# A fused attention and token-mixing kernel: a new table for the order of issue and for who copies

## The chip, the core and the metric

The kernel runs on one core of a Trainium2 chip. A core has a matrix engine (PE, with weight loads shown apart as PEld), a vector engine (DVE), a scalar engine (ACT), GpSimd (POOL), and a queue on SyncE (SP) that starts the transfers. Each engine works through its own instructions strictly in the order in which they were issued, and semaphores tie the engines together. The metric is the time of one execution on the device in microseconds (us). The kernel before took 118.97 us in the median of three runs (117.5 to 119.05).

## The reference

```python
# q, k, v: (8, 8, 576, 64) float32; w_q, w_k: (512, 64); w_out: (512, 512)
def phi(x, c, s):                        # c, s: cos and sin of pi/2 * position / 576
    r = np.maximum(x, 0.0)
    return np.concatenate([r * c, r * s], axis=-1)
q_p, k_p = phi(q, cos_w, sin_w), phi(k, cos_w, sin_w)
kv  = np.einsum('bhsf,bhsd->bhfd', k_p, v)
z   = np.sum(k_p, axis=2)
x   = np.einsum('bhsf,bhfd->bhsd', q_p, kv) / (np.einsum('bhsf,bhf->bhs', q_p, z)[..., None] + 1e-6)
x   = x.transpose(0, 2, 1, 3).reshape(8, 576, 512)
W   = (1 / 8) * np.einsum('bsd,btd->bst', x @ w_q, x @ w_k)
out = np.maximum(np.einsum('bst,btd->bsd', W, x), 0.0) @ w_out      # float32, (8, 576, 512)
```

## The kernel before

The eight batches are cut into sixteen half batches H of four heads. Everything is written out by hand: a table of words, `ORDER`, is read from front to back, and each word issues one step. A word has the step's name, its number, after a colon the bank of the accumulator memory (PSUM, eight banks; for output copies the number of one of sixteen output buffers), and after an @ the engine: A is ACT, V is DVE, G is POOL. So `RQ2@A` is the relu of q for half batch 2 on ACT. A final a or b means one half of the step's data. An engine's order is the order of its words; words on different engines bind each other through data and buffers alone.

The steps of a half batch H:

- LV, LK, LQ load v, k and q, 288 KB for each half (line 137, SP); four buffers for each of the three.
- RK, RQ: relu and cast of k and q (line 202 on ACT, 204 on POOL). CV: cast of v (208 on ACT, 210 on POOL). VS: v times the cos and sin tables, on DVE from CV's result (line 236) or on POOL straight from the loaded v (line 233).
- KV or KU: the product of k and v on PE (lines 258 and 284), KE copies it out (lines 208 on ACT, 212 on DVE).
- QT or QU: transposition of q on PE, in 18 narrow or 9 wide matmuls (lines 269 and 276); QM multiplies it by the tables on DVE (lines 303 and 300, the latter twice for each QU).
- N (two for each H): numerators and denominators on PE (line 319). EJ adds epsilon, RC takes the reciprocal (line 338), X divides on DVE (line 344, two for each H).
- XT or XR: x transposed on PE, in 10 wide or 20 narrow matmuls (lines 367 and 380); XE copies it out. On ACT this copy moves two bf16 at a time as one float32 word; on DVE it moves bf16.

The steps of a batch b: WK and WQ project x (lines 403 and 416), KW and QW copy the results; KX multiplies by x (line 506), XK copies the result out, XA and XB copy it across the two halves of the partitions (each 64x256). MX (four for each batch, two matmuls, line 535) mixes the tokens, ME applies the relu (line 526 on ACT, 528 on DVE). Batches 4 and 5 go through a joint variant (WC, QC, WT, KC, KP, XP, MP, MM). For two batches together there are nine output tiles: WO is four matmuls of 512 columns (line 552), OE copies the bank out (208 on ACT, 212 on DVE), ST stores 256 KB (line 562, SP).

At the start stand the tables: TQ, TK and TI on POOL, TV and TW (sine by ACT, lines 167 and 182; TV makes the small table for v, TW the one for q), TP and T2 copy TV's table (lines 172 and 186), TZ sets edges of buffers to zero in eight memsets (lines 190 to 195). LW loads and CW casts the weights.

v's scaled copies have two buffers, so VS of H waits for KV of H-2; the loads wait for the relu or cast that empties their buffer.

Of the kernel before, what the change touches and what calls it, by code (L numbers as in the profile page):

```python
# [21 lines left out]


ORDER = """
LV1a LK1a LQ1b LV1b TI TQ TZ0@G TK LQ1a TV T2 TP0 CV1a@A RQ1b@G TW LK1b RQ1a@A CV1b@G VS1a@V
VS1b@V RK1a@G RK1b@A QT1:0 LV0a LQ0b LQ0a LV0b LK0a LK0b LV2a LV2b CV0a@A LK2a LK2b LQ2b QM1 LQ2a
KV1:2 CV0b@G KE1@A LQ3b LQ3a LW0 LW1 N3:2 LV3a LV3b N2:0 LK3b VS0a@V LK3a LV4b LV4a VS0b@V RQ0a@A
LQ4a RQ0b@A RK0a@G LQ4b RK0b@G EJ1@A LK4a LQ5a LK4b LQ5b LW2 CV2@G LV5a LW3 LW4 LW5 LV5b LK5b
LK5a RC1 QU0:4 KV0:6 QM0 KE0@A X2 X3 N1:6 RK2@G N0:4 EJ0@A VS2@V RQ2@A RC0 XR1:2 XE1@A RQ3@G X0
KU2:0 QT2:4 X1 XT0:6 XE0@A CW1@A KE2@V QM2 QU3:0 CW0@V N5:4 N4:6 CV3@G RK3@G QM3 LV6b LQ6a LV6a  # L30
LK6b LQ6b VS3@V EJ2@V WK0:2 KW0@A WQ0:3 QW0@A KX0:2 RC2 X5 LK6a KV3:0 XK0@A XA0@A VS4@G MX1:2
XB0@A KE3@A ME1@A RQ4@A X4 MX0:4 ME0@V LV7b N6:0 N7:2 RQ5@G EJ3@V MX3:6 XT2:4 ME3@A RK4@A RC3
QT4:6 X7 XE2@A X6 XT3:0 KV4:2 KE4@A QM4 XE3@V QU5:6 WK1:0 N8:2 QM5 CW2@G CW4@G CW5@G KW1@A MX2:4
N9:0 EJ4@V CW3@G ME2@A RC4 CV5@G KX1:6 WQ1:7 X8 WO3:4 WO2:5 QW1@A XK1@A WO1:6 X9 VS5@V OE2:0@V
OE1:1@V XB1@A OE3:2@A XA1@A MX6:0 RK5@G MX5:4 KV5:2 ME5@V ME6@A MX7:6 MX4:0 KE5@A LQ7a ME7@A LV7a
LK7b LQ8a LQ7b ME4@V LV8b LK7a N10:2 N11:4 LV8a LQ8b EJ5@V RC5 XR4:6 WO0:0 WO6:1 X10 XE4@A CV6@G
RQ6@G RK6@G WO5:6 X11 QU6:4 OE0:3@A OE5:4@A OE6:5@A VS7@G VS6@V QM6 KV6:2 XT5:6 WO8:1 KE6@V XE5@V
N12:2 N13:4 WO7:0 RQ7@A OE8:6@V EJ6@V RC6 WK2:1 RK7@A KW2@A RQ8@A LV9a LK8b LQ9b LK8a LV10b LQ9a
QT7:6 X13 LV9b OE7:7@V LK9b LK9a LV11b LQ10b LQ10a QM7 WQ2:4 LV10a LQ11a LK11b LK10b LK10a LQ11b
LV11a KV7:0 LK11a KE7@A VS8@G QU8:6 X12 KX2:5 N15:2 XK2@A RK8@A N14:0 QM8 EJ7@V WO4:5 RC7 X14  # L40
KU8:6 X15 XB2@G XA2@G OE4:8@A QW2@A KE8@A MX8:4 MX9:0 ME8@A ME9@V XR6:2 RQ9@G XR7:6 XE7@V QU9:0
XE6@A N16:4 N17:6 WK3:2 WQ3:3 QM9 RK9@A KW3@A VS9@G EJ8@V RC8 RQ10@A KX3:2 XK3@A XB3@A MX10:0
QW3@A X16 KU9:4 KE9@A X17 ME10@V MX11:2 MX15:0 N19:4 N18:6 ME11@A ME15@V WO11:2 EJ9@V XA3@A
MX12:0 WO12:3 RC9 X18 LQ13b LV13b RK10@A LV13a LK12a LQ12b LK13a LQ13a MX13:6 LV12b LK14a LK14b
LK12b ST2 ST6 LV12a LK13b LQ12a X19 MX14:4 OE12:9@V OE11:10@A ME12@A VS10@G KV10:0 ME13@A ME14@V
XR9:2 XE9@V RQ11@G QT11:6 QT10:4 QM10 KE10@A RK11@A XT8:0 XE8@A QM11 WO16:2 VS11@G WO15:3 N20:0
OE15:11@A N21:4 EJ10@A OE16:12@V KV11:6 RC10 X21 RQ13@G WO13:2 KE11@A N22:6 X20 N23:4 WO14:3
EJ11@V WO9:0 OE13:13@A LV15a ST12 LV14b ST3 LK15b ST15 LQ14b LV15b RC11 OE14:14@A XR10:2 LK15a
LQ14a LQ15b ST8 ST13 ST5 ST16 LQ15a X23 X22 QT13:4 OE9:15@A XR11:6 XE11@V WC4:0 XE10@A WC5:6
VS13@G QC4@A QC5@V WO17:0 RQ12@A QT12:2 WT2:6 RK13@A KC2@A WO10:1 KP2:6 OE17:0@V QM13 KV13:4  # L50
OE10:5@A XP2@A KE13@A MP22:6 MP20:0 QM12 MP23:2 RK12@G VS12@G MM22@A KV12:4 MP19:6 MM23@A MM20@V
VS15@G MP16:0 KE12@V MP21:2 MM16@V MM19@A MM21@A N24:4 N25:6 MP18:0 EJ12@A MM18@A WO26:2 OE26:9@A
ST14 LV14a ST17 WO21:0 RC12 X25 X24 N26:2 MP17:6 N27:4 OE21:2@A WO25:0 MM17@V EJ13@A RQ14@A RC13
RK15@G X26 OE25:11@V X27 ST7 ST21 RQ15@G RK14@G WO24:6 WO22:2 OE24:6@A VS14@G KV15:6 QT15:4
OE22:13@V ST22 ST4 ST26 ST1 ST0 QT14:2 QM15 KE15@A QM14 XR13:6 WO19:0 WO18:1 XE13@A XR12:6 N30:4
N31:2 OE19:4@A XE12@V EJ15@V OE18:12@A KV14:0 KE14@A WK6:6 RC15 X31 X30 N29:0 N28:2 KW6@A WQ6:6
KX6:7 EJ14@V QW6@A XK6@A WO23:4 XA6@G RC14 X29 X28 XR14:2 XR15:6 XE14@A XB6@A MX24:0 OE23:14@V
WO20:5 ME24@A XE15@V WK7:4 KW7@A MX27:2 OE20:0@V ME27@A MX26:0 MX25:6 ME25@V ME26@A WQ7:5 KX7:4
XK7@A QW7@A XB7@G XA7@A WO29:0 WO27:1 MX30:4 OE29:7@V MX28:6 MX31:2 WO30:0 OE27:2@A ME28@A ME31@V
ST18 ST24 ST25 MX29:6 ST10 ST9 ST23 ME29@A ME30@V ST11 WO28:1 WO34:6 ST27 ST29 ST20 OE28:13@V  # L60
OE30:8@A OE34:9@A ST19 WO35:0 WO33:1 WO31:6 OE31:1@A ST30 ST28 WO32:4 ST34 OE35:3@V OE32:12@A
ST35 OE33:6@V ST33 ST31 ST32
"""


# [566 lines left out]
```

## Time and profile before

| | |
|---|---|
| median of 3 runs | 118.97 us |
| the profiled execution | 119.31 us, span 117.0 us, mean granted PE clock 0.978 |
| busy in the span | PE 95.5, PEld 63.4, DVE 87.5, ACT 68.7, POOL 74.3 us |
| moved by the transfers | 39.36 MB, 336 GB/s over the span; 29.62 MB read, 9.44 MB written |
| chain that ended last | PE 67%, transfers 11%, DVE 6%, ACT 4% |

The span is the time from the first to the last instruction; the execution's own time is 2.3 us longer. Rows of groups give the line, the engine, the operation, what it writes and reads, the count, the busy time and the mean of one in ns. Rows of a timeline give the start, the duration, the engine, the line and the operation, and in brackets how long the engine sat idle ahead of it and what released it. Rows of the chain give start, duration and what the end was waiting for then.

### The profile page before, as it was taken

To read this page: it belongs to the slowest core of one execution; us is meant where nothing else is said; L and a number is where in the kernel's file an instruction comes from. 1 tells how busy PE (TensorE), PEld (TensorE's weight loads), DVE (VectorE), ACT (ScalarE), POOL (GpSimd) and SP (SyncE) were. 2 spreads that over 40 slices of the span, in tenths; PEclk is the share of its full clock that TensorE was granted. 3 is DMA by queue.
4 is the path that set the end of the run, shared out by engine and by line. 5 is a ranking of instruction groups with operands and counts; after the bars stand their busy time and mean duration, and the time that the engine had idled before them with its cause. 6 is when DMAs were issued, how large, how long until landed. Compare 5 with 4: busy or idle time off the path is not lost.

```text
span 117.0 us, 4959 instructions
## 1 busy us (share of the span) xinstructions
PE 95.5 (82%) x2124; PEld 63.4 (54%) x2138; DVE 87.5 (75%) x132; ACT 68.7 (59%) x120; POOL 74.3 (63%) x72
## 2 busy tenths in 40 slices
PE   0018746998799999988887988999999999999970
PEld 0017544875684657675754555484555668563420
DVE  0336897898989899988795986948779899846330
ACT  4457215359736656748788944469786454585540
POOL 7461670579876779879999955999499950110000
PEclk9999998599999999999999999999999999999997
DMA  3999999999999999999999999999993179731994
GB/s 99 294 387 412 392 384 330 380 391 390 389 392 390 391 385 385 381 388 384 395 384 391 390 385 387 395 393 385 397 391 137 52 277 370 269 124 49 381 382 174
DMA packets 20660, 39.36 MB, mean 336 GB/s; under 512 B 3232, under 2 KB 3232, under 8 KB 20640
## 3 DMA queue, kind: packets, MB, share of 16 engines
q1 hardware_dynamic: 20640, 39.07, 91.0%
q8 instruction: 16, 0.26, 0.9%
q14 instruction: 4, 0.03, 0.1%
HBM read 29.62 MB, written 9.44 MB: 334 GB/s over the span
## 4 chain that ended last, share of the span: by engine, by line
PE 67%; DMA 11%; DVE 6%; issue 5%; ACT 4%; SPq 4%; DVEq 0%; ACTq 0%
PE ps L552 27%; PE ps L319 8%; DMA qraw<-in_q_dram 6%; DMA vraw<-in_v_dram 5%; PE ps L258 5%; SPq L137 4%; DVE x L344 3%; PE ps L380 3%; PE ps L276 3%; PE ps L367 3%; PE ps L403 3%; PE ps L506 3%; PE ps L535 3%; PE ps L269 3%; PE ps L416 3%
## 5 line engine op out<-in xcount | busy, mean ns | idle before, releaser
L233 POOL TENSOR_TENSOR v<-vraw,vtab 128x1152 bf16<-128x1152 f32 x20 | 42.1, 2130 | 4.7 <-PE ps L258 3.1
L552 PE MATMUL ps<-wow,mix 128*128 128x512 bf16 x130 | 33.4, 380 | 1.2 <-DVE o L212 0.4
L344 DVE TENSOR_TENSOR x<-ps,rec 128x640 bf16<-128x640 f32 x32 | 25.1, 819 | 0.7
L552 PEld LDWEIGHTS <-mix 128*128 128x128 bf16 x144 | 12.7, 98 | 14.7 <-issue 1.3
L208 ACT COPY o<-ps 128x512 f32<-128x512 f32 x21 | 12.2, 585 | 10.9 <-PE ps L552 10.9
L319 PE MATMUL ps<-kvs,qm 64*128 64x65 bf16 x640 | 14.2, 195 | 1.8 <-ACT kvs L208 1.6
L319 PEld LDWEIGHTS <-qm 64*128 64x128 bf16 x640 | 12.5, 97 | 5.5 <-issue 4.1
L303 DVE TENSOR_TENSOR qm<-ps,qtab 128x2304 bf16<-128x2304 bf16 x10 | 13.3, 1353 | 2.0 <-PE ps L269 2.0
L212 DVE COPY o<-ps 128x512 f32<-128x512 f32 x15 | 10.2, 688 | 4.6 <-PE ps L552 3.8
L269 PE MATMUL ps<-ident,rq 64*128 64x64 bf16 x180 | 4.6, 199 | 10.6 <-POOL rk L204 8.4
L204 POOL TENSOR_SCALAR rq<-qraw 128x1152 bf16<-128x1152 f32 (+1 forms) x8 | 8.7, 1087 | 7.1 <-DMA qraw<-in_q_dram 5.6
L526 ACT ACTIVATE mix<-ps 128x576 bf16<-128x576 f32 x19 | 12.0, 650 | 1.7 <-PE ps L535 1.4
L202 ACT ACTIVATE rq<-qraw 128x1152 bf16<-128x1152 f32 (+1 forms) x10 | 10.1, 1019 | 4.9 <-DMA qraw<-in_q_dram 4.9
L528 DVE TENSOR_SCALAR mix<-ps 128x576 bf16<-128x576 f32 x13 | 9.7, 753 | 3.1 <-PE ps L535 2.1
L258 PE MATMUL ps<-v,rk 64*64 64x130 bf16 x468 | 10.3, 227 | 0.8 <-issue 0.4
L204 POOL TENSOR_SCALAR rk<-kraw 128x1152 bf16<-128x1152 f32 (+1 forms) x10 | 10.0, 1004 | 1.0 <-PE ps L403 0.4
L236 DVE TENSOR_TENSOR v<-vb,ps 128x1152 bf16<-128x1152 bf16 (+1 forms) x8 | 8.4, 1051 | 2.6 <-POOL vb L210 2.5
L208 ACT CAST kvs<-ps 128x260 bf16<-128x260 f32 (+1 forms) x13 | 5.3, 411 | 8.3 <-PE ps L258 7.0
L210 POOL TENSOR_SCALAR vb<-vraw 128x1152 bf16<-128x1152 f32 (+1 forms) x6 | 6.0, 993 | 6.5 <-DMA vraw<-in_v_dram 6.4
L258 PEld LDWEIGHTS <-rk 64*64 64x64 bf16 x468 | 7.9, 110 | 3.8 <-issue 2.4
L269 PEld LDWEIGHTS <-rq 64*128 64x128 bf16 x180 | 3.6, 100 | 11.6 <-POOL vb L210 8.4
L300 DVE TENSOR_TENSOR qm<-ps,qtab 128x1152 bf16<-128x1152 bf16 x12 | 8.5, 752 | 1.3 <-PE ps L276 1.1
(63 smaller groups left out, 126.4 us busy)
## 6 DMA issues: line engine op xcount, KB each, us to landing
vraw<-in_v_dram SPq DMA_DIRECT2D x32, 288.0 KB, 5.9
kraw<-in_k_dram SPq DMA_DIRECT2D x32, 288.0 KB, 5.9
qraw<-in_q_dram SPq DMA_DIRECT2D x32, 288.0 KB, 5.9
...
```

The source lines that it names most:

```text
L202: A.activation(dst, s, AF.Relu)
L204: eng.tensor_scalar(dst, s, FMAX, 0.0, op0=ALU.min, op1=ALU.max)
L208: A.copy(dst, s)
L212: V.tensor_copy(dst, s)
L233: G.tensor_tensor(o[:, :, :, s].rearrange("p r c d -> p (r c) d"), v, vtab[:, 0:n * C, s, 0:1].to_broadcast([P, n * C, D]), op=ALU.mult)
L258: nc.tensor.matmul(kv_v[o, r, :], rk_b[H % NPREP][a, c, pr, :], v2_b[H % NV2][a, pr, c, :, 0:D + 1], start=(c == 0), stop=(c == C - 1))
L269: nc.tensor.transpose(qt_v[:, r, c * H2:(c + 1) * H2], rq_b[H % NPREP][a, c, :, :], ident[a, a])
L303: V.tensor_mul(qm_b[H % NQM][:, :, :, 0:C, :].rearrange("p s r c d -> p s r (c d)"), qt_view(at).unsqueeze(1).to_broadcast([P, 2, 2, S]), ...
L319: nc.tensor.matmul(nv[:, pr, u, :], qm_b[H % NQM][a, s, r, 2 * u:2 * u + 2, :], kv_b[H % NKV][a, r, pr if place["KV", H][1] else 0, s, 0:D ...
L344: V.tensor_tensor(x_b[b % NX][:, :, 4 * h:4 * h + 4, :].rearrange("p u (w r) d -> p r w u d", r=2)[:, r], num(place["N", g])[:, :, :, 0:D] ...
L526: A.activation(dst, s, AF.Relu, scale=scale_moe)
L552: nc.tensor.matmul(o, mix_b[bp % 2][:, m, rt * P:(rt + 1) * P], wow[:, m, :], start=(m == 0), stop=(m == NDM - 1))
```

## The change

Only the table `ORDER` is replaced. The computation, the buffers and the code of the steps stay. The table again has 598 words. All steps are there again, and 14 transpositions change their kind (QT3, QT5, QT9 for QU3, QU5, QU9; QU4, QU7, QU10, QU11 for QT4, QT7, QT10, QT11; XT1, XT6, XT9 for XR1, XR6, XR9; XR0, XR3, XR8 for XT0, XT3, XT8), so there are 7 QU instead of 6 and still 11 XR and 5 XT. Of the copies out, XE is on ACT 15 times (before 9), OE 26 times (before 21), KW 3 times (6), QW 4 times (6); RQ is on POOL 10 times (8). VS stays 8 times on DVE and 10 on POOL, but VS6 is now on POOL and VS9 on DVE, so CV6 goes and a CV9 on ACT comes. The first and the last lines of the diff:

```diff
-LV1a LK1a LQ1b LV1b TI TQ TZ0@G TK LQ1a TV T2 TP0 CV1a@A RQ1b@G TW LK1b RQ1a@A CV1b@G VS1a@V
+TQ TI LK1b LV1a LQ1a TK RQ1a@G LV1b RK1b@G CV1a@A TV TW LQ1b CV1b@A TP0 TZ0@V T2 VS1b@V VS1a@V
...
-ST35 OE33:6@V ST33 ST31 ST32
+ST33 OE32:2@A ST34 OE35:1@V ST35 ST32
```

**First place: the start of ACT's program.** vb is what CV writes, vtab is TV's table, qtab TW's; rq and rk are what RQ and RK write; kvs is KE's. Before:

```order
L167 ACT_TABLE_LOAD
L167 ACTIVATE vtab_129<-ki_128 128x72
L208 CAST vb1_82<-vraw1_72 128x576
L182 ACTIVATE qtab_130<-wof_135 128x1152
L202 ACTIVATE rq1_79<-qraw1_68 128x9x64
L202 ACTIVATE rk1_76<-kraw1_64 128x9x64
L208 CAST vb0_81<-vraw0_71 128x576
L208 CAST kvs1_89<-ps_127 128x2x2x65
```

Now, at the same place:

```order
L208 ACT_TABLE_LOAD
L208 CAST vb1_82<-vraw1_72 128x576
L167 ACT_TABLE_LOAD
L167 ACTIVATE vtab_129<-ki_128 128x72
L182 ACTIVATE qtab_130<-wof_135 128x1152
L208 CAST vb1_82<-vraw1_72 128x576
L202 ACTIVATE rq0_78<-qraw0_67 128x9x64
L208 CAST kvs1_89<-ps_127 128x2x2x65
```

CV1a now stands ahead of TV, and ACT loads its function tables twice: once for the cast, once more behind it for the sine. CV1b has come to ACT, the relus RQ1a and RK1b have gone to POOL.

**Second place: the start of DVE's program.** v20 and v21 are the two buffers of scaled v, qm is QM's result, rec the reciprocals, x X's result. Before:

```order
L186 COPY v20_84<-vtab_129 128x36x2
L186 COPY v21_85<-vtab_129 128x36x2
L172 COPY ps_127<-vtab_129 128x36
L236 TENSOR_TENSOR v21_85<-vb1_82,ps_127 128x18x64 x2
L303 TENSOR_TENSOR qm1_87<-ps_127,qtab_130 128x4x576
```

Now:

```order
L172 COPY ps_127<-vtab_129 128x36
L190 MEMSET qm0_86 128x4x32
L190 MEMSET qm1_87 128x4x32
L192 MEMSET xT0_98 128x4x32
L192 MEMSET xT1_99 128x4x32
L192 MEMSET xT2_100 128x4x32
L194 MEMSET qk0_137 128x32
L194 MEMSET qk1_138 128x32
L195 MEMSET eps_132 128x1
L186 COPY v20_84<-vtab_129 128x36x2
L186 COPY v21_85<-vtab_129 128x36x2
L236 TENSOR_TENSOR v21_85<-vb1_82,ps_127 128x18x64 x2
```

The eight memsets of TZ have moved from POOL to DVE, between the table's copy and the first product with v. They do not wait for that product's data.

**Third place: the middle of ACT's program, around batches 2 and 3.** rk2 from kraw0 is RK8, xT0 is XE6 and later XE7, wq0 is QW2, kx0 is XK2 (a cast) and XA2 and XB2 (copies of 64x256), kvs2 is KE8, kvs0 KE9, mix1 is ME. Before:

```order
L208 CAST kx0_106<-ps_127 128x256
L202 ACTIVATE rk2_77<-kraw0_63 128x2x9x64
L208 COPY o8_119<-ps_127 128x512
L208 CAST wq0_104<-ps_127 128x288
L208 CAST kvs2_90<-ps_127 128x8x65
L526 ACTIVATE mix1_110<-ps_127 128x576
L208 COPY xT0_98<-ps_127 128x2x2x5x32
L202 ACTIVATE rk0_75<-kraw1_64 128x2x9x64
```

Now:

```order
L208 COPY o8_119<-ps_127 128x512
L208 COPY xT0_98<-ps_127 128x2x288
L208 CAST wq0_104<-ps_127 128x288
L202 ACTIVATE rk2_77<-kraw0_63 128x2x9x64
L208 COPY kx0_106<-kx0_106 64x256 x2
L208 COPY xT0_98<-ps_127 128x2x2x5x32
L208 CAST kvs2_90<-ps_127 128x8x65
L526 ACTIVATE mix1_110<-ps_127 128x576 x2
```

RK8 stood ahead of QW2 and now stands behind it; XA2 and XB2 have come from POOL, XE6 stands ahead of QW2 and XE7 ahead of KE8, while RK9 (rk0) has left for POOL.

More of the change, by code (lines that the diff above doesn't have):

```diff
@@ L24 @@
 ORDER = """
-LV1a LK1a LQ1b LV1b TI TQ TZ0@G TK LQ1a TV T2 TP0 CV1a@A RQ1b@G TW LK1b RQ1a@A CV1b@G VS1a@V
[L26 to L60, printed above, removed]
@@ L61 @@
-OE30:8@A OE34:9@A ST19 WO35:0 WO33:1 WO31:6 OE31:1@A ST30 ST28 WO32:4 ST34 OE35:3@V OE32:12@A
-ST35 OE33:6@V ST33 ST31 ST32
+TQ TI LK1b LV1a LQ1a TK RQ1a@G LV1b RK1b@G CV1a@A TV TW LQ1b CV1b@A TP0 TZ0@V T2 VS1b@V VS1a@V
+RQ1b@G LK1a QT1:0 RK1a@G LQ0b LQ0a LV0b LV0a LK0b CV0b@G CV0a@G LK0a LV2b LV2a LK2b LK2a QM1
+KV1:2 RQ0b@A KE1@A RQ0a@A LQ2a LQ2b LV3a LV3b LQ3b LW1 LK3b LQ3a RK0a@A LW0 LK3a RK0b@G LV4b LV4a
+VS0b@V LK4a LW2 LQ4b LQ4a CV2@G N3:2 RK2@G LV5a LK4b LQ5a LQ5b LW5 LV5b LW3 RQ2@G LW4 LK5a LK5b
@@ new lines @@
+N2:0 EJ1@V RC1 VS0a@V QU0:4 QM0 KV0:6 KE0@A X3 N0:6 X2 N1:4 VS2@V LV6a LV6b CW1@G CV3@G EJ0@V
+XT1:0 XE1@A RC0 X1 KU2:2 X0 QT2:0 KE2@A XR0:6 XE0@A QM2 RQ3@G VS3@V CW0@G RK3@G WK0:6 N5:0 KW0@A
+KX0:6 XK0@A XB0@A QT3:2 QM3 N4:4 VS4@G KV3:6 EJ2@A RC2 X4 KE3@A XA0@A RK4@G WQ0:2 RQ5@G X5 N6:6
+QW0@A LQ7a LQ6a LQ6b LK6b LK6a LV7b N7:4 MX2:2 ME2@A EJ3@V RC3 CW5@G X7 MX1:0 RQ4@A CV5@G XT2:2
+X6 MX3:4 XR3:6 LV7a LK7b LQ7b LK7a XE2@A XE3@A ME1@V LQ8b QU4:2 QM4 LQ8a ME3@A MX0:0 ME0@A WK1:6
+KV4:4 KW1@V QT5:2 KX1:6 KE4@A LV8b LV8a QM5 WQ1:7 QW1@V N8:4 N9:2 CW2@A CW3@A EJ4@A VS5@V RC4
@@ new lines @@
+XK1@A CW4@G X9 WO3:0 X8 WO1:1 OE1:0@A OE3:1@V RK5@G XB1@G KV5:6 XA1@A MX4:2 KE5@A LV9b LV9a MX6:4
+MX5:6 WO0:1 ME5@A VS6@G ME4@V ME6@V MX7:2 OE0:2@A N11:6 RQ6@A N10:4 ME7@V RK6@A XR4:0 WO5:2 WO2:3
+EJ5@V RC5 X11 QU6:6 LQ9b X10 OE2:3@A XE4@A LK8b RK7@A OE5:4@V LQ9a RQ7@A LK8a QM6 KV6:4 KE6@V
+XT5:2 WO7:0 OE7:5@V N13:4 N12:6 EJ6@V RC6 X12 WO6:1 X13 VS7@G WO8:0 OE8:6@V QU7:6 OE6:7@A KV7:4
+XE5@A LV10b LK9b LQ10b RQ8@G LK9a LQ10a QM7 QU8:2 LK10b LV10a KE7@A VS8@G WK2:0 N14:6 QM8 KW2@A
+CV9@A N15:4 EJ7@V WO4:0 XT6:2 RQ9@G RK9@G LK10a LQ11b LV11a LQ12a WQ2:1 OE4:8@A KX2:0 XE6@A RC7
@@ new lines @@
+X14 QW2@A X15 XK2@V RK8@A XA2@A XB2@A XR7:4 QT9:0 VS9@V KU8:2 QM9 RQ10@G XE7@A MX8:6 KE8@A WK3:4
+N17:2 KW3@V ME8@A N16:0 EJ8@V RC8 MX11:4 KU9:6 X17 X16 ME11@A WQ3:4 KE9@A QW3@V MX10:2 ME10@A
+N19:6 MX9:0 N18:4 EJ9@V ME9@A KX3:2 RK10@A WO11:3 WO12:0 LQ11a LV11b XK3@A RC9 LV13a LK11b LQ13a
+LK11a XB3@A X18 X19 LQ14b VS10@G OE11:9@V ST4 ST2 LV12b LQ12b LV12a LQ13b LK13a LV13b LK13b XA3@A
+MX15:6 MX13:4 ME15@V KV10:2 KE10@V OE12:10@A RQ11@G VS11@G ME13@A MX14:0 XR8:6 MX12:4 ME12@V
+QU11:2 ME14@A QU10:0 QM10 WO15:4 XE8@A RK11@A WO16:5 XT9:0 QM11 OE15:11@A OE16:12@A XE9@A N20:6
@@ new lines @@
+N21:4 EJ10@V KV11:2 RC10 KE11@A X20 X21 WO13:0 N22:6 N23:2 WO9:1 OE13:13@A EJ11@V RC11 RQ13@A
+WC4:4 OE9:14@A XR10:0 LQ15a LV15b ST0 LQ15b LV14b LV14a ST8 LK12a LK12b X23 LK14a LK14b LV15a
+ST13 ST16 ST3 LK15b LK15a ST7 LQ14a ST5 ST12 ST15 RQ12@G VS12@G X22 XR11:6 QC4@V XE10@A QT13:2
+WO14:4 ST11 XE11@V WC5:6 WO17:5 QM13 QC5@V QT12:2 WT2:6 KC2@V RK13@A VS13@G RK12@G OE14:15@A QM12
+OE17:8@A RQ15@A WO10:4 KP2:5 OE10:3@A KV13:2 XP2@A MP22:4 KE13@A MP20:6 MM22@A MM20@V MP16:0
+MM16@A KV12:2 MP23:4 KE12@V MP21:6 MM21@V MM23@A MP19:0 MM19@A N25:2 N24:4 MP18:6 MM18@A EJ12@V
@@ new lines @@
+RC12 WO21:0 X25 WO26:1 X24 MP17:2 N27:6 OE21:2@A OE26:6@A N26:4 QT15:0 EJ13@A MM17@V WO25:2
+WO24:3 RC13 RK15@A RQ14@A X27 X26 OE24:13@A OE25:12@A VS15@G WO19:6 QM15 KV15:4 KE15@A ST14
+XR13:2 OE19:1@V ST24 ST6 ST17 QT14:0 XE13@A N31:4 N30:6 RK14@G VS14@G EJ15@A WO18:2 WO22:3 QM14
+RC15 OE18:5@A X30 X31 OE22:4@A KV14:0 XR12:6 XR15:4 KE14@V XE12@A N29:0 N28:2 EJ14@V WK6:6 RC14
+X29 WQ6:7 KW6@A X28 QW6@A KX6:6 XE15@A XK6@A XA6@G WO23:0 XR14:6 MX24:4 OE23:10@V ME24@V XE14@A
+XB6@A WO20:2 WK7:3 MX25:4 MX27:6 KW7@V OE20:11@A ME27@A ME25@V MX26:0 WQ7:2 ME26@A KX7:3 WO28:0
@@ L63 @@
+WO27:1 OE27:9@V XK7@A XA7@A QW7@A XB7@G MX28:2 MX29:4 MX31:6 OE28:15@A ME29@A ME28@V ME31@A
+WO29:0 MX30:4 ME30@A WO30:1 WO31:4 OE30:13@A OE29:7@V WO33:5 OE31:8@A WO34:4 ST10 ST23 WO35:1
+ST21 ST19 ST22 ST1 ST26 ST25 ST18 OE33:3@A ST27 ST28 ST9 ST20 WO32:5 ST30 OE34:10@A ST31 ST29
+ST33 OE32:2@A ST34 OE35:1@V ST35 ST32
 """
```

## The prediction

> **What bounds the kernel now.** I read the page first: busy shares, the granted clock, the share of the transfers, and the chain that ended last.
>
> ```profile
> PE 95.5 (82%) x2124; PEld 63.4 (54%) x2138; DVE 87.5 (75%) x132; ACT 68.7 (59%) x120; POOL 74.3 (63%) x72
> DMA  3999999999999999999999999999993179731994
> PE 67%; DMA 11%; DVE 6%; issue 5%; ACT 4%; SPq 4%; DVEq 0%; ACTq 0%
> ```
>
> PE carries two thirds of the chain, while the transfers run at nine tenths or more for the first three quarters of the span. Averages over such different parts hide where time could be won, so I then cut the span by hand, at the changes of the granted clock and at the last matmul. The columns are busy time and count of PE, PEld, DVE, ACT and POOL, the clock, the transfers' share, and GB/s.
>
> ```profile
> 19.83:23.25 3.42, 3.42 (x66) 2.99 (x67) 2.34 (x3) 1.38 (x3) 1.61 (x2) 0.50 1.05 384
> 23.25:31.00 7.75, 6.47 (x178) 4.83 (x172) 7.31 (x13) 6.06 (x11) 6.69 (x5) 1.00 1.05 390
> 31.00:68.00 37.00, 34.01 (x810) 23.00 (x814) 32.69 (x52) 25.09 (x43) 32.38 (x24) 1.00 1.05 388
> 68.00:113.40 45.40, 44.01 (x877) 26.09 (x878) 33.67 (x48) 26.66 (x51) 23.49 (x16) 1.00 0.79 296
> ```
>
> From 23.25 us to its last matmul PE is idle for 1.28 + 2.99 + 1.39 = 5.66 us of 90.15. That is all that an order of issue can win there, and 2% of the time is 2.4 us. Ahead of it PE has gaps, and from 19.83 to 23.25 it runs at half clock: work of about 1.7 us takes 3.4.
>
> The Trainium skill, "TensorE: Matmul & The Clock Gate", section "What's actually happening", says that a free-running window of about 3.4 us decides the clock, so that the cold stretch depends on where the windows fall. The 3.42 us at 0.50 fit it; whether another start warms PE sooner no row here shows.
>
> **The change, part by part.**
>
> *A. The start.* The first place of the change shows a second table load, between CV1a and TV.
>
> ```profile
> 0.73 1.28 ACT L167 ACT_TABLE_LOAD   x1 [0.73 <-PEq L616]
> 4.46 0.26 ACT L167 ACTIVATE vtab<-ki 128x72 bf16<-128x72 int32 x1 [2.45 <-POOL ki L161]
> 4.63 0.65 ACT L208 CAST vb<-vraw 128x576 bf16<-128x576 f32 x1
> 5.19 1.16 ACT L182 ACTIVATE qtab<-wof 128x1152 bf16<-128x1152 int32 x1
> 6.21 0.67 POOL L204 TENSOR_SCALAR rq<-qraw 128x576 bf16<-128x576 f32 x1 [1.78 <-DMA qraw<-in_q_dram]
> 2.94 0.82 POOL L192 MEMSET xT<- 128x256 bf16 x3
> ```
>
> Before, the load (1.28 us) ran while nothing else could, and TV waited for POOL's ki until 4.46. LV1a was the first transfer and had landed by 4.63, the third released POOL at 6.21. LV1a is now second: I place its landing midway, at 5.4. Then CV1a ends at 6.1, the second table load at 7.4, TV at 7.6, TW at 8.75, CV1b at 9.4. DVE has its tables from 7.6, so TZ's memsets have 1.8 us less the copies of the table; I count them hidden. At POOL's price they would stick out: three of the eight take 0.82 there, by which all eight come to some 1.7 to 2. So v's first product on DVE starts at s = 9.4. With the landing at 4.63 s would be 8.6; at 6.21 with the memsets at POOL's price, 10.8.
>
> The section "What ACT_TABLE_LOAD costs" of the Trainium skill's page "ScalarE: Activation LUTs" adds a drain of 1.38 us to each switch of sets. By it s would be 10.8 already with the middle landing; the row above shows the load alone, 1.28.
>
> What hangs on s, until QM2:
>
> ```profile
> 8.98 1.25 PE L258 MATMUL ps<-v,rk 64*64 64x130 bf16 x36
> 10.70 1.28 PE L319 MATMUL ps<-kvs,qm 64*128 64x65 bf16 x40 [0.48 <-ACT kvs L208]
> 9.16 1.36 DVE L303 TENSOR_TENSOR qm<-ps,qtab 128x2304 bf16<-128x2304 bf16 x1 [0.74 <-PE ps L269]
> 12.05 0.75 DVE L236 TENSOR_TENSOR v<-vb,ps 128x1152 bf16<-128x1152 bf16 x1 [0.87 <-POOL vb L210]
> 19.09 0.69 DVE L212 CAST kvs<-ps 128x520 bf16<-128x520 f32 x1
> 20.40 1.36 DVE L303 TENSOR_TENSOR qm<-ps,qtab 128x2304 bf16<-128x2304 bf16 x1 [0.61 <-PE ps L269]
> ```
>
> From QM1 to QM2 DVE took 20.40 - 9.16 = 11.24 us. Of these 0.87 was a wait for POOL's vb, 0.61 a wait for QT2, and 0.69 KE2, which is on ACT now: 9.07 stay. Two EJ come to DVE (0.4 with their hand-over), and EJ1 waits for N2: two products with v (1.4), KV1 (1.25), KE1 (0.4), N3 and N2 (1.3) put its start at s + 4.4, while DVE is free at s + 3.35, so 1.05 more. QM1 itself starts at s + 1.4. QM2 then starts at 9.4 + 1.4 + 9.07 + 0.4 + 1.05 = 21.3, that is 0.9 late. Behind it stand XR0 (0.8 at half clock), XE0 (0.7), WK0 (0.7), N5 (0.5), KX0 (0.65), QT3 (0.4) and N4 (0.5), and KV3 could start at 25.6. But it couldn't start sooner anyway:
>
> ```profile
> 24.30 1.15 POOL L204 TENSOR_SCALAR rk<-kraw 128x1152 bf16<-128x1152 f32 x1 [0.37 <-PE ps L403]
> 29.41 0.44 PE L269 MATMUL ps<-ident,rq 64*128 64x64 bf16 x18 [0.45 <-ACT mix L526]
> 30.42 0.73 PE L367 MATMUL ps<-ident,x 128*128 128x128 bf16 x10 [0.57 <-DVE x L344]
> 31.08 0.72 PE L258 MATMUL ps<-v,rk 64*64 64x130 bf16 x36
> ```
>
> RK3 ended at 25.45, and LK3a is the 26th transfer in both orders. So the late start is swallowed by the wait for k, up to s = 9.4, and beyond it each microsecond counts in full. On the other side KV4 began at 31.08. Now WQ0 (0.6) is left for behind KV3; X7 and X6 end at 30.2 as DVE adds up (QM3 to 26.4, RC2, X4, X5 to 28.3, EJ3, RC3, X7, X6), where PE waits 1.0 instead of the 0.45 + 0.57 above; then XR3, QU4, MX0 and WK1 bring KV4 to 32.1. That is 1.0 late, with more work done.
>
> ```profile
> 57.90 0.69 PE ps L403 x20
> 68.29 0.67 PE ps L367 x10
> 66.61 0.40 PE ps L380 x20
> 31.80 0.61 PE ps L276 x9
> 48.42 0.37 PE ps L269 x18
> ```
>
> WK1 (0.69) and a further MX (0.24) are done by then that stood behind KV4 before; one of the wide transpositions of x has yet to come (0.67 - 0.40 = 0.27 to pay back), and over the whole kernel one QT became a QU (0.61 - 0.37 = 0.24). So **A = 1.0 - 0.69 - 0.24 + 0.27 + 0.24 = +0.6 us**. Its ends: -1.5, if QM2 isn't late and the half clock of 19.83 to 23.25 mostly goes; +2.0 with s = 10.8.
>
> *B. Two waits of PE that go.*
>
> ```profile
> 61.98 0.60 ACT kvs L208
> 62.63 0.80 PE L319 MATMUL ps<-kvs,qm 64*128 64x65 bf16 x40 [0.44 <-ACT kvs L208]
> 72.50 1.02 PE L552 MATMUL ps<-wow,mix 128*128 128x512 bf16 x3 [0.45 <-DVE o L212]
> 52.28 1.17 ACT L202 ACTIVATE rk<-kraw 128x1152 bf16<-128x1152 f32 x1
> 58.59 0.61 PE ps L416 x8
> ```
>
> N19 waits for KE9 (0.60), and between KU9 and N19 stood two MX only. Now WQ3 (0.61) and MX10 (0.24) stand there and cover it: -0.44. WO13 waited for bank 2, which OE16 on DVE freed late. Now it uses bank 0, last freed by XE9 on ACT, with N20, N21 and KV11 (about 1.4) between: -0.45. What is late next there is PE itself. **B = -0.9 us**, between 0 and -0.9.
>
> *C. Waits that come.* The third place of the change: RK8 (1.17) now stands behind QW2 (0.40), and KU8 needs it. From WQ2's end that is 1.66 with the hand-overs, while KX2, XR7 and QT9 fill 1.44: 0.2. XA2, XB2 and XE7 behind RK8 end 1.5 after it, KU8 and MX8 fill 1.35, so WK3 waits 0.15 to 0.2. Around batch 3, RK10, XK3, XB3 and XA3 stand in a row on ACT and take until 2.25 after KX3, where WO11 and WO12 fill 1.95, and MX13 waits for 0.2. **C = +0.6 us**, between 0 and 1.5, since I followed the likeliest places and not all.
>
> *D. Copies that change engines.* Per copy ACT is the faster one:
>
> ```profile
> L526 ACT ACTIVATE mix<-ps 128x576 bf16<-128x576 f32 x19 | 12.0, 650 | 1.7 <-PE ps L535 1.4
> L528 DVE TENSOR_SCALAR mix<-ps 128x576 bf16<-128x576 f32 x13 | 9.7, 753 | 3.1 <-PE ps L535 2.1
> ```
>
> By such means, step by step, ACT gets some 4 us more work and DVE some 4 less. ACT with 73 of 117 us and DVE with 84 stay below PE, so this counts only through A to C: 0.
>
> The Trainium skill, "ScalarE: Activation LUTs", section "Rules for kernel authors", says to use VectorE and not ScalarE for a relu. The trace disagrees for these shapes read from PSUM (650 ns against 753); by the rule the move would cost time.
>
> *E. The end.*
>
> ```profile
> 83.77 30.57 SPq L562 DMA_DIRECT2D out_dram<-o  x26
> 113.39 0.59 ACT o L208
> 114.00:115.00 1.00, 0.00 (x0) 0.00 (x0) 0.00 (x0) 0.00 (x0) 0.00 (x0) 1.00 0.92 338
> ```
>
> The end is PE's last tile, its copy and its store, with the transfers still busy. In the new order eight stores instead of ten stand ahead of the last load, and then SP waits for WO24's and WO23's tiles with others ready behind them: nineteen stores are left when WO23 is copied, 11.7 us ahead of PE's end (its successors' work: 6 tiles at the end, 4 more, one batch's WK, WQ, KX, MX). At 256 KB and 385 GB/s each takes 0.68 us, together 12.9: they end 1.2 us behind PE, and the last store of 113.39 + 0.59 has to go out later than that in any case. **E = 0**, up to +0.5.
>
> The sum is 119.31 + 0.6 - 0.9 + 0.6 = 119.6 us against the profiled execution. That one lay 0.34 above the median of the runs, so **119.3 us** is the forecast, which is no change within what a measurement of this kernel can tell, about 2%.
>
> **Rivals.**
>
> *Slower: the second table load is not swallowed.* From s = 9.4 on each microsecond on ACT goes through DVE's queue into QM2, N4 and KV3. At s = 10.8 that is 1.4 more: 120.7 us, slower than before; with C at its end of 1.5 it is 121.6. For it: DVE is busy 2.34 of 3.42 in that stretch and can't catch up. Against: POOL's RK3 bounds KV3 from the other side. The drain that the Trainium skill gives would make this the likeliest case.
>
> *Faster: the cover is better than I count.* If s is 8.6 or PE is warm from 19.83 on, A turns to -1.5, and with C at 0 the sum is 119.3 - 2.1 - 0.6 = 116.6. Against: PE waits for data there, and warm matmuls wait sooner.
>
> *The bound moves to the stores.* If SP is held up longer at WO23, each store left costs 0.68: three more give 121.3. For it: one queue in order. Against: nineteen times 0.68 still ends ahead.
>
> **How the numbers follow.** Forecast 0.62, slower start 0.18 (half of it beyond 2%), faster 0.12, stores 0.08. The range of 117.0 to 121.9 leaves out about 0.15: it reaches down almost to the faster case and takes in both slower ones. Slower by over 2% (above 121.35): 0.09 from the start, 0.03 from the stores, 0.05 from the forecast's own edge, 0.17. Faster by over 2% (below 116.6): most of the faster case and a little of the forecast's edge, 0.11. Within: 0.72.
>
> **What would show it.** A: a second ACT_TABLE_LOAD behind CV1a, DVE's first product with v near 9.4, QM2 near 21.3, KV4 near 32. B: N19 and WO13 without a wait. C: waits of 0.2 ahead of KU8, WK3 and MX13. E: the transfers idle between 93 and 101, then busy to the end. The forecast falls if PE idles over 7 us behind 23.25, or if KV3 starts behind 26.5.

## The result, and the profile after

The changed kernel takes 118.44 us (median of 20 runs, 116.51 to 120.02) against 119.07 us (20 runs, 117.47 to 122.43): 0.63 us less. The ratio, from which disturbed runs are left out, is 0.9896 [0.9856, 0.9937]. So it is faster by 0.5% in the medians of all runs and by 1% in the ratio: less than 2%, but more than the comparison is uncertain by, where I had forecast no change. The profiled execution took 117.42 us with a span of 115.4 us; before it was 119.31 and 117.0.

First the page, in the lines that were shown of before:

```profile
PE 95.5 (83%) x2129; PEld 63.3 (55%) x2129; DVE 83.0 (72%) x138; ACT 73.9 (64%) x124; POOL 72.7 (63%) x64
DMA  3999999999999999999999999999996450199994
PE 64%; DMA 25%; ACT 4%; issue 1%; SPq 1%; POOL 1%; POOLq 0%
```

PE's busy time is the same. In the chain, "issue" went from 5% to 1%: time in which the engine that the chain is on stands still with nothing that the profile shows to wait for. Of before's 5%, 2.15 us are four halts of PE, which come below. Then the windows, cut as before (the last one ends 0.2 us behind the last matmul):

```profile
19.83:23.25 3.42, 2.26 (x70) 1.89 (x70) 2.13 (x3) 1.12 (x2) 2.19 (x3) 1.00 1.10 363
23.25:31.00 7.75, 5.39 (x169) 4.02 (x167) 6.34 (x10) 4.94 (x10) 7.37 (x6) 1.00 1.04 385
31.00:68.00 37.00, 35.85 (x809) 24.60 (x808) 32.64 (x54) 27.54 (x47) 31.86 (x22) 1.00 1.04 386
68.00:111.80 43.80, 43.44 (x862) 25.41 (x860) 30.18 (x47) 30.87 (x54) 20.95 (x13) 1.00 0.81 304
```

Before 31 us PE does less than before: 5.39 us busy of 7.75, where it was 6.47. Behind 31 us it is idle for 1.15 + 0.36 = 1.51 us, where it was 2.99 + 1.39 = 4.38. The 2.87 us that are won there are three times the two waits that I had counted on (0.9). The profile lists no stretch at half clock between 15 and 114 us, where that of before had one at 19.83 to 23.25. The two profiles differ by more (1.9 us) than the medians (0.63), but that stretch doesn't account for it: KV4 starts at 31.08 in before and at 31.94 here, so what is won is won behind it.

The start, in rows of the timeline of after:

```profile
4.32 0.67 ACT L208 CAST vb<-vraw 128x576 bf16<-128x576 f32 x1 [2.30 <-DMA vraw<-in_v_dram]
5.00 1.28 ACT L167 ACT_TABLE_LOAD   x1
6.30 0.26 ACT L167 ACTIVATE vtab<-ki 128x72 bf16<-128x72 int32 x1
8.21 1.42 DVE L236 TENSOR_TENSOR v<-vb,ps 128x1152 bf16<-128x1152 bf16 x2 [0.32 <-ACT vb L208]
19.81 1.36 DVE L303 TENSOR_TENSOR qm<-ps,qtab 128x2304 bf16<-128x2304 bf16 x1
25.70 0.72 PE L258 MATMUL ps<-v,rk 64*64 64x130 bf16 x36 [1.17 <-POOL rk L204]
31.94 0.72 PE L258 MATMUL ps<-v,rk 64*64 64x130 bf16 x36
```

v's first product starts at 8.21 instead of my 9.4, QM2 at 19.81 instead of 21.3 (before 20.40). KV3 waits for POOL's rk all the same, for 1.17 us, and KV4 starts at 31.94, where I had put it at 32.1.

The places of the steps B, C and E, from the timeline, the last copy from the chain:

```profile
54.79 0.44 PE L269 MATMUL ps<-ident,rq 64*128 64x64 bf16 x18 [0.19 <-DVE kx L212]
60.36 0.47 PE L319 MATMUL ps<-kvs,qm 64*128 64x65 bf16 x20
70.64 1.04 PE L552 MATMUL ps<-wow,mix 128*128 128x512 bf16 x4
111.63 0.58 ACT o L208
```

N19 (60.36) and WO13 (70.64) start without a wait. QT9 (54.79) has a new one of 0.19. The last copy is at 111.63, and was at 113.39.

**Where the rest came from.** Before's chain of waits has four halts marked "issue" in the middle of a step. These are the rows behind them:

```profile
50.09 0.60 PE L258 MATMUL ps<-v,rk 64*64 64x130 bf16 x28 [0.45 <-issue]
55.88 0.55 PE L380 MATMUL ps<-ident,x 64*128 64x64 bf16 x25 [0.55 <-issue]
61.54 0.40 PE L284 MATMUL ps<-v,rk 64*128 64x260 bf16 x4 [0.57 <-issue]
67.73 0.55 PE L269 MATMUL ps<-ident,rq 64*128 64x64 bf16 x26 [0.58 <-issue]
```

(The rows of XR6 and QT11 run on into XR7 and QT10, which stand right behind them.) KV7 halts with 8 of its 36 products done, XR6 with 15 of its 20 transpositions, KU9 with 14 of 18, QT11 with 10 of 18: 0.45 + 0.55 + 0.57 + 0.58 = 2.15 us, each inside a step whose operands are all there. After's chain has one such halt:

```profile
37.73 0.71 PE L258 MATMUL ps<-v,rk 64*64 64x130 bf16 x34 [0.49 <-issue]
```

and a second of 0.10 at 72.00, in N22. So 2.15 - 0.59 = 1.56 of the 2.87 us are halts that are gone, 0.89 are the waits of N19 and WO13, and the rest is small waits.

The halts have a period. Each matmul is a weight load and a multiplication, two instructions of PE. Counted through the order from the first, the halts of before fall on instructions 1726, 1981, 2237 and 2493: 255, 256 and 256 apart. The two of after fall on 1214 and 2750, two pages ahead of 1726 and one page behind 2493 (512 and 257 instructions). The windows between before's halts, and the queue on the page that carries instructions:

```profile
50.09:55.88 5.79, 5.19 (x127) 3.74 (x127) 5.03 (x9) 3.71 (x7) 4.93 (x5) 1.00 1.05 386
55.88:61.54 5.66, 5.09 (x129) 3.85 (x130) 4.74 (x8) 4.34 (x8) 5.66 (x4) 1.00 1.05 388
61.54:67.73 6.19, 5.12 (x127) 3.03 (x128) 4.73 (x8) 5.46 (x9) 6.19 (x4) 1.00 1.05 391
q8 instruction: 16, 0.26, 0.9%
```

127 + 127, 129 + 130 and 127 + 128 instructions: 256 within the few records that are missing or blurred at the cuts. The queue moved 16 packets, 0.26 MB, so 16 KB in each. PE has 2 x 2138 = 4276 instructions, and 4276 / 256 = 16.7: a packet is a page of PE's program. (After has 4258: thirteen transpositions change their kind, not the 14 that I counted ahead of the prediction.) The experiments bear this out: the three kernels below whose PE program has 4334 instructions or more moved 17 packets within the span, all others 16. The packets' own records in the trace of before are:

```
halt ends   next packet starts   has landed   next halt ends
  50.09            53.49            54.45          55.88
  55.88            59.17            60.28          61.54
  61.54            65.38            66.49          67.73
```

From one end of a halt to the packet's start it is 3.3 to 3.8 us, the packet takes 1.0 to 1.1, and PE goes on 1.2 to 1.4 after it has landed. Together 5.7 to 6.2 us for a page, and PE's work in it was 5.1 to 5.2. The reading: **a page of 256 instructions that holds less work than its successor's fetch takes ends in a halt.** The experiments test that.

### The profile page after: what moved, and what is told of

The parts are those of the page before. It is cut to its first block, busy times and chain, and to the rows that moved or that the text cites. A ratio compares the mean times of both kernels' runs of the same rounds, so it can differ in the third digit from the quotient of the medians.

```text
span 115.4 us, 4951 instructions
## 1 busy us (share of the span) xinstructions
PE 95.5 (83%) x2129; PEld 63.3 (55%) x2129; DVE 83.0 (72%) x138; ACT 73.9 (64%) x124; POOL 72.7 (63%) x64
## 4 chain that ended last, share of the span: by engine, by line
PE 64%; DMA 25%; ACT 4%; issue 1%; SPq 1%; POOL 1%; POOLq 0%
PE ps L552 29%; DMA vraw<-in_v_dram 15%; PE ps L319 7%; DMA kraw<-in_k_dram 5%; PE ps L258 5%; DMA qraw<-in_q_dram 5%; PE ps L535 3%; PE ps L276 3%; PE ps L380 2%; PE ps L416 2%; PE ps L403 2%; PE ps L506 2%; PE ps L441 2%; PE ps L367 2%; PE ps L269 1%
## 5 line engine op out<-in xcount | busy, mean ns | idle before, releaser
L552 PE MATMUL ps<-wow,mix 128*128 128x512 bf16 x144 | 34.7, 380 | 0.0
L208 ACT COPY o<-ps 128x512 f32<-128x512 f32 x26 | 15.1, 584 | 8.7 <-PE ps L552 8.7
L204 POOL TENSOR_SCALAR rq<-qraw 128x1152 bf16<-128x1152 f32 (+1 forms) x10 | 10.5, 1050 | 6.4 <-DMA qraw<-in_q_dram 6.2
L208 ACT COPY xT<-ps 128x640 f32<-128x640 f32 (+1 forms) x15 | 10.1, 674 | 4.8 <-PE ps L380 2.9
L303 DVE TENSOR_TENSOR qm<-ps,qtab 128x2304 bf16<-128x2304 bf16 x9 | 12.2, 1352 | 1.0 <-PE ps L269 1.0
L212 DVE COPY o<-ps 128x512 f32<-128x512 f32 x10 | 6.9, 686 | 7.6 <-PE ps L552 5.2
L258 PEld LDWEIGHTS <-rk 64*64 64x64 bf16 x468 | 8.4, 114 | 5.9 <-issue 2.5
L300 DVE TENSOR_TENSOR qm<-ps,qtab 128x1152 bf16<-128x1152 bf16 x14 | 9.7, 748 | 1.1 <-PE ps L276 1.1
L528 DVE TENSOR_SCALAR mix<-ps 128x576 bf16<-128x576 f32 x12 | 9.0, 753 | 2.1 <-PE ps L486 1.5
L202 ACT ACTIVATE rk<-kraw 128x1152 bf16<-128x1152 f32 (+1 forms) x8 | 8.8, 1103 | 1.6 <-DMA kraw<-in_k_dram 1.6
```

What stands on the lines that cost most here:

```text
L202: A.activation(dst, s, AF.Relu)
L204: eng.tensor_scalar(dst, s, FMAX, 0.0, op0=ALU.min, op1=ALU.max)
L208: A.copy(dst, s)
L258: nc.tensor.matmul(kv_v[o, r, :], rk_b[H % NPREP][a, c, pr, :], v2_b[H % NV2][a, pr, c, :, 0:D + 1], start=(c == 0), stop=(c == C - 1))
L300: V.tensor_mul(qm_b[H % NQM][:, s, :, 0:C, :], q, qtab[:, s].unsqueeze(1).to_broadcast([P, 2, C, H2]))
L303: V.tensor_mul(qm_b[H % NQM][:, :, :, 0:C, :].rearrange("p s r c d -> p s r (c d)"), qt_view(at).unsqueeze(1).to_broadcast([P, 2, 2, S]), ...
```

## Experiments

The theory: the halts come from the fetch of PE's program, page by page, and the change gained because fewer of its pages run out. The rivals: the gain lies in the start and its tables; it is the waits of step B alone; and a halt belongs to the step in which it stands, so that steps cost what their matmuls take.

### The pages of before, moved by 160 and by 256 instructions

A step of small products that nothing reads is put at the head of PE's program, where PE waits for data anyway. 80 of them are 160 instructions, 128 are 256.

```diff
+    def PD(i, ps, eng):
+        for _ in range(i):
+            nc.tensor.matmul(bank(2)[:, 0:64], ident, ident[:, 0:64], start=True, stop=True)
-LV1a LK1a LQ1b LV1b TI TQ ...
+LV1a LK1a LQ1b LV1b TI PD80 TQ ...      (PD128 in the second kernel)
```

> The kernel before, with 80 small matmuls (128x64 on the identity, results never read) at the start of PE's program, where PE has nothing to do until 8.4 us. They move every later PE instruction 160 rows on, so that the page boundaries (every 256 rows) fall elsewhere: in N7, N8, N11, N12, N15, N16, WO11, N20 instead of KV3, KV4, KV5, KV6, KV7, XR6, KU9, QT11. Theory 1 (what the change won is mostly PE's halts at page boundaries, 0.45 + 0.55 + 0.57 + 0.58 = 2.15 us in the kernel before): the four halts at KV7, XR6, KU9 and QT11 go, at most two others of 0.5 come, and the time falls by 1 to 2 us (ratio 0.985 to 0.99) with nothing else changed. Rival (the halts are waits for something else at those steps, and what the change won are the two waits of N and WO for copies): the four halts stay at KV7, XR6, KU9 and QT11, ratio 1.00.

> The same with 128 small matmuls, 256 rows, one whole page: the boundaries fall in the same steps as in the kernel before. A control for what the small matmuls do by themselves (a warmer clock at the start, or a later QT1). Theory 1: the halts at KV7, XR6, KU9 and QT11 are there again with 0.45 to 0.6 each, and the time is that of the kernel before within 0.5% (ratio 0.995 to 1.005), unless the matmuls reach past 8.4 us, which would show at QT1. Rival (the small matmuls themselves help, by the clock): it is as fast as the kernel with 80 of them.

With 80: 119.32 us against 119.70, ratio 1.0027 [0.9973, 1.008]. The four halts at KV7, XR6, KU9 and QT11 are gone, and others stand at N7 (0.86), N16 and WO11, on instructions 959, 2237 and 2493 of the longer program: the same places of the page as before, in other steps. A row of the timeline and one of the chain:

```profile
58.72 0.58 PE L319 MATMUL ps<-kvs,qm 64*128 64x65 bf16 x26 [1.25 <-issue]
64.10 0.81 issue
```

And the queue that carries instructions:

```profile
q8 instruction: 17, 0.28, 1.0%
```

So the place follows the count of instructions, not the step. The time did not follow: 0.86 + 1.25 + 0.81 = 2.9 us of halts are no less than the 2.15 of before. The gain that I expected was a miss.

With 128: 120.17 us, 1.0079 [1.0022, 1.0137]. Of the four halts only one came back at its place, at KU9:

```profile
61.64 0.90 issue
```

That is a miss for the other three, and for the time, which is 0.8% longer where I expected none. A boundary is where a halt can stand, and whether it does hangs on when its page was fetched, which differs between kernels and executions. Nor are the two times a clean measure of the halts: the small products go with a slower PE clock at the start (mean clock over the runs 0.957 and 0.955, of before 0.990). With 80 it was at half from 8.56 to 11.97 and from 18.80 to 22.21 us, with 128 from 13.77 to 24.01, in before from 19.83 to 23.25.

### The changed kernel with one table load

```diff
-... RK1b@G CV1a@A TV TW LQ1b ...
+... RK1b@G TV CV1a@A TW LQ1b ...
```

> The changed kernel with TV moved ahead of CV1a, so that ACT loads its function tables once. By the step of the prediction that priced the start: DVE's first product with v starts about 1.3 us sooner than the 8.21 of the changed kernel, QM2 up to 1 us sooner, but KV3 still waits for RK3 (25.7), so the end moves by 0 to -0.4 us (ratio to before 0.985 to 0.99). If the second load is paid in full it is 1.3 us faster than the changed kernel (ratio about 0.98).

118.09 us against 119.70, 0.9966 [0.9918, 1.0014], against after's own 0.9896: no gain. The second load is gone, but v's first product comes only 0.42 us sooner (7.79 instead of 8.21, where I had expected 1.3), since it waits for CV1b; QM2 comes no sooner (20.23), and KV3 starts when rk is there, after the same wait:

```profile
26.08 0.72 PE L258 MATMUL ps<-v,rk 64*64 64x130 bf16 x36 [1.17 <-POOL rk L204]
```

So the second table load costs nothing at the end. That the rest of the start gains nothing isn't tested by itself; KV4, which comes later in after than in before, speaks against it.

### Before with one copy moved

```diff
-OE15:11@A N21:4 EJ10@A OE16:12@V ...
+OE15:11@A N21:4 EJ10@A OE16:12@A ...
```

> The kernel before with one word changed: OE16 on ACT instead of DVE. By the step of the prediction on the two waits, WO13 no longer waits 0.45 us for DVE's copy (72.5 us in the kernel before), and the matmuls end up to 0.4 us sooner. If the wait is not DVE's queue but the copy itself, some 0.3 us of it stay.

118.69 us in a single run, span 116.7, at full clock from 21.49 us on (ahead of it PE's matmuls take as long as at half clock: KU2 2.13 us, against 1.19 in before). WO13's wait falls from 0.45 us to 0.20. The halts stand at the same four places, with other lengths, 2.55 us in all:

```profile
49.10 0.32 issue
54.66 0.82 issue
60.57 0.56 issue
66.75 0.85 issue
```

This part of B is worth 0.25 us by itself, by these two profiles. A second execution of nearly the same program has its halts in the same places, with other lengths.

### Before with fewer instructions, after with more

XT and QU transpose in wide tiles of 128x128, XR and QT the same data in 64x64 halves, with twice the instructions. The first edit takes 78 instructions out of before and adds some 1.05 us of matmul time; the second adds 76 to after and takes some 1.0 us away.

```diff
 before: XR4:6 -> XT4:6, XR6:2 -> XT6:2, XR7:6 -> XT7:6, QT7:6 -> QU7:6
 after:  XT5:2 -> XR5:2, XT6:2 -> XR6:2, QU7:6 -> QT7:6, QU8:2 -> QT8:2
```

> The kernel before with four of PE's steps made wider between 41 and 66 us: XT4, XT6, XT7 for XR4, XR6, XR7 and QU7 for QT7. PE then has 78 instructions fewer there, but about 3 x 0.27 + 0.24 = 1.05 us more matmul time. Theory 1, as the first runs have sharpened it (while the transfers are saturated, PE gets its next 256 instructions only some 5.8 us after the last page's start, so poor pages end in a halt): the halts of that stretch (2.1 to 2.5 us in all) shrink by 1 us or more, the matmuls do not end later, ratio 0.99 to 1.00. Rival (PE's matmul time bounds that stretch, and the halts cost what they cost at each boundary): 1.05 us slower, ratio 1.009.

> The reverse in the changed kernel: XR5, XR6 for XT5, XT6 and QT7, QT8 for QU7, QU8, which gives PE 76 instructions more between 43 and 54 us and about 1.0 us less matmul time. Theory 1: what is saved in matmuls is lost again in halts at the boundaries of rows 1470 to 2750 (0.1 us of idle PE in the changed kernel, then 1 us or more), ratio to the changed kernel 1.00 to 1.005, that is 0.985 to 0.995 to the one before. Rival (matmul time bounds): 0.6 to 1 us faster than the changed kernel.

Before with wider tiles: 118.12 us against 118.83, 0.9969 [0.9927, 1.0011], and so not slower by its longer matmuls, as it would be if these alone counted (1.05 / 118.83 = 0.9%). Its window:

```profile
31.00:68.00 37.00, 36.15 (x802) 24.89 (x801) 33.27 (x54) 25.47 (x44) 32.02 (x24) 1.00 1.05 389
```

PE is busy for 36.15 of 37.00 us, where it was 34.01, and from 33 us on no halt is left in PE's rows. What it wins in halts it pays in part with longer matmuls; the last copy starts at 112.67, before at 113.39.

After with narrower tiles: 122.55 us, 1.0345 [1.0281, 1.0409] against before. The changed kernel took 117.89 us in the same set, so the edit cost 4.66 us, or 4%. This is far more than I expected. The timeline row behind the longest halt, the window of that halt, and the one behind it, at half clock:

```profile
55.09 0.23 PE L380 MATMUL ps<-ident,x 64*128 64x64 bf16 x3 [1.88 <-issue]
53.10:56.50 3.40, 1.52 (x34) 1.13 (x29) 0.97 (x2) 1.51 (x4) 1.48 (x2) 1.00 1.04 387
56.50:59.90 3.40, 3.38 (x60) 2.50 (x59) 2.95 (x3) 2.46 (x5) 1.38 (x3) 0.50 1.05 388
```

Three halts of 0.41, 1.88 and 0.76 us, at 49.02, 53.20 and 95.08, two short ones of 0.17 and 0.24 behind 78 and 100 us, and behind the long one a window of 3.4 us at half clock. So 76 instructions more, with less matmul time, cost 4.66 us. In this profile the halts are 3.46 us against 1.43 in the second profile of after, which is shown below, and the half clock makes at most 1.7 (an estimate: half of the 3.4). The clock isn't needed for the loss, though: three of the six runs had a mean clock above 0.99 and took 121.8 to 122.4 us. The theory gives the direction of this edit, and the matmuls' time does not; the size it had not given. Of the first edit the runs say only that it isn't slower by its matmuls, not that it is faster.

### Before with half of the loads

> The kernel before without the loads of q, k and v for the half batches 8 to 15 (it computes on what the buffers still hold), so that the transfers are idle from about 50 us on apart from stores. PE's program is the same, word for word. Theory 1: the fetch of a page takes about 1 us then instead of 2.5 to 3.8, and the halts at KU9 and QT11 (0.57 and 0.58) are gone, those at KV7 and XR6 as far as the loads have ended by then. Rival (each boundary costs PE's sequencer a fixed time that only long matmuls hide): all four stay at 0.45 to 0.6 us.

In `load`, which issues the loads of q, k and v:

```diff
+        if H >= 8:
+            return
```

118.93 us in a single run. Behind 50 us the transfers are idle, and PE's window there can be laid beside that of before. First this kernel, then before:

```profile
50.00:68.00 18.00, 17.52 (x452) 12.32 (x451) 16.45 (x27) 14.32 (x25) 14.64 (x10) 1.00 0.01 3
```

```profile
50.00:68.00 18.00, 15.66 (x400) 10.89 (x403) 14.81 (x25) 13.78 (x23) 17.14 (x11) 1.00 1.05 389
```

In the same 18 us PE issues 452 matmuls instead of 400, with the same program (the windows hold partly different steps), and the four halts are gone. The packets start 0.4 to 1.3 us behind the boundary there, not 3.3 to 3.8. From the instruction of KV7's halt to that of QT11's it takes 15.96 us, where it took 17.64: 1.68 less, about the three halts in between. This is the strongest run for the theory: without the other transfers the fetch comes early and the halts are gone. The total is hardly less than the 119.31 of before's profiled execution: both had one stretch at half clock, KV4 starts 0.66 us later here (31.74 against 31.08), and this one has a halt of its own in KV6, just as the loads ran out:

```profile
45.23 1.41 issue
```

One relation holds in all thirteen profiles. Take each boundary's packet and the first weight load behind the boundary: of 198 boundaries PE passes none sooner than 1.2 us after the packet has landed. And every halt marked "issue" of more than 0.16 us in PE's rows stands at a boundary, within two matmuls of the count, and ends 1.2 to 1.6 us after the landing. This ties the halts to the arrival of the page; a wait for something else in those steps would have no reason to end there.

### The changed kernel once more

> The changed kernel unchanged, on the same chip as the kernels of this call, for their comparison and a second profile. Both theories: ratio 0.985 to 0.995 to the kernel before; halts of PE behind 31 us 0.4 to 0.9 us in all, and no wait ahead of N19 and WO13.

No edit. 117.89 us against 118.83, 0.9932 [0.9892, 0.9972]: faster again, in another set of runs. The gain isn't PE's clock: among the runs that the ratio uses, those with a mean clock above 0.99 have medians of 118.55 us (10 of before) and 117.76 (8 of after). N19 and WO13 have no wait in this execution either. Its halts in the chain:

```profile
49.10 0.39 issue
60.22 0.56 issue
66.69 0.29 issue
```

With one of 0.19 at KV5 they are 1.43 us, in KV7, WQ3, QU11 and KV5, all on boundaries of the same pages; the first profile of after had 0.59. The kernel with one table load, whose PE program is the same, has three in PE's rows, 0.89 us in all. So by these profiles the gain in halts is between 0.7 (1.43 against 2.15) and 2.0 us (0.59 against 2.55), and the first profile of after was at the favourable end.

### Wider tiles in both

Three kernels look for a version that beats both: after with three wide steps, that with one table load too, and before with the four wide steps and the copy of above.

```diff
 after:  XR4:0 -> XT4:0, XR7:4 -> XT7:4, QT9:0 -> QU9:0
 after, second: the same, and TV ahead of CV1a@A
 before: XR4:6 -> XT4:6, XR6:2 -> XT6:2, XR7:6 -> XT7:6, QT7:6 -> QU7:6, OE16:12@V -> OE16:12@A
```

> The changed kernel with XT4, XT7 for XR4, XR7 and QU9 for QT9: 58 PE instructions fewer between 41 and 56 us, about 2 x 0.27 + 0.24 = 0.8 us more matmul time. Theory 1: the halts at the boundaries of rows 1214 to 2494 (0.6 to 1.3 us in the changed kernel) go to 0.3 us or less, so it ends within 0.5 us of the changed kernel, ratio to before 0.985 to 0.995. Rival (matmul time bounds): 0.8 us slower than the changed kernel, ratio about 1.00.

> The same with TV ahead of CV1a, one table load. Theory: the start is bounded by the loads of k, so nothing changes at the end beyond 0.3 us; ratio to before 0.985 to 0.995. If the second table load was paid after all: up to 1 us faster than the kernel above.

> The kernel before with XT4, XT6, XT7, QU7 and OE16 on ACT: no halts and no wait ahead of WO13. Theory 1: as fast as the changed kernel, ratio to before 0.985 to 0.995, with five words of the table changed. Rival (the rest of the new order matters): it stays at the 0.997 of the four wide steps alone.

118.37, 119.24 and 118.31 us against 119.10 (medians of all runs); ratios 1.0002 [0.9961, 1.0043], 1.0014 [0.9955, 1.0073] and 1.0009 [0.9968, 1.0051]. None is established as faster than before, and none comes out better than after did (0.9896 and 0.9932); all three were expected at 0.985 to 0.995. The halts didn't all go: the first still has 0.43 at KV5 and 0.46 in WO9, the second 0.97 behind 61 us:

```profile
61.37 0.97 issue
```

The first has four halts of 0.1 us or more, 1.23 us in all, which lies between after's 0.59 and 1.43: its wider tiles lengthen the matmuls and take away no halts that can be seen. The third has no halt above 0.16 us in PE's rows; by the ratio it is no faster for it, by the medians 0.8 us faster, so what that is worth stays open. A count of 256 isn't enough to place a halt; I did not find a rule by which to lay an order out so that none occurs.

## Why the prediction was wrong, point by point

**The step that failed is the first one, the sum's base.** That PE is idle for 5.66 us from 23.25 us to its last matmul was right. But I quoted the page's "issue 5%" and gave it no term. The sum started from the profiled 119.31, and so carried over 2.15 us of halts as if they belonged to the kernel; they belong to the order, since they hang on which steps share a page. That term should have read -0.7 to -2.0, by the two profiles of after against the two of before's order. Four rows of the same form, "issue" inside a step and 5.7 to 6.2 us apart, stood in before's timeline for anyone who looked for what they have in common.

The Trainium skill, "Runtime: NRT & Kernel Launch", section "Instruction fetch mechanics", says that an engine's program comes in blocks of 16 KiB, 256 instructions, over a queue of its own, and that crossing a boundary is mostly hidden. The traces agree on the size (16 packets, 0.26 MB). "Mostly hidden" holds for the count, since twelve of before's sixteen boundaries show no halt, but not for the cost where the transfers are busy: 0.1 to 1.9 us in a boundary that halts.

**A, the start, +0.6.** The parts were off and mostly cancelled. s was 8.21: LV1a had landed by 4.3, not 5.4, and TV followed the second load at once (5.00 + 1.28, then 6.30), so the drain of 1.38 us by the Trainium skill's "ScalarE: Activation LUTs", section "What ACT_TABLE_LOAD costs", wasn't there. QM2 at 19.81 was 1.5 ahead of my 21.3. That did not matter, as step A said: KV3 was bound by RK3 on POOL. KV4 came at 31.94 (32.1 foretold), and the waits ahead of it were 0.48 and 0.28. The run with one table load bears out that the load is swallowed, and the slower rival fell with it.

**B, -0.9: right.** N19 and WO13 wait for nothing, in both profiles of after.

**C, +0.6: too much.** Nothing waits at KU8 or MX13; QT9 waits for 0.19 and WK3 for 0.13, in all 0.3.

**D, 0.** ACT is busy for 73.9 instead of 68.7, DVE for 83.0 instead of 87.5, about what was foretold, and PE is still the bound.

**E, 0: right.** The transfers nearly stop between 95 and 100 us and are busy to the end:

```profile
95.00:100.00 5.00, 5.00 (x135) 3.40 (x128) 3.22 (x7) 3.00 (x6) 0.40 (x1) 1.00 0.09 32
100.00:105.00 5.00, 4.99 (x61) 2.85 (x59) 1.85 (x4) 3.92 (x9) 0.40 (x1) 1.00 0.86 320
```

and from the start of the last copy to the end of the span it is 115.4 - 111.63 = 3.8 us, before 117.0 - 113.39 = 3.6.

**The sum without the halts.** Taking each execution's halts from the start of its last copy gives 111.63 - 0.59 = 111.04 and 112.42 - 1.43 = 110.99 for after. The same for before's order is 113.39 - 2.15 = 111.24 in its own profile, and 113.00 - 2.55 + 0.25 = 110.70 in the run with one copy moved, the 0.25 being that copy's. So the rest of the change costs between -0.2 and +0.3 us, near the sum of A, B and C with the 0.3 that C came to (0.6 - 0.9 + 0.3 = 0). This leans on four profiles, in which KV4 starts anywhere from 30.4 to 32.0 us, and is an estimate. By this estimate the forecast missed by a term that it did not have, not by those that it had. The faster rival had the direction, but its mechanism, a warm PE and better cover, is not the one that the runs showed.

**What stays open.** Why a fetch starts 3.3 to 3.8 us behind the boundary under load, and what PE does in the 1.2 to 1.4 us behind its landing. How the gain splits between the halts and the two waits of B: no run measures it, and the split above is worked out from profiles that, of one PE program, differ by up to 0.8 us in their halts. And the total: in the runs with halts removed (wider tiles in before) or moved, part of the time was there again in other places, so the halts explain the difference between these two kernels better than they serve as a lever.
